# The matmuls of two dense layers as pairs on 64-column tiles of the array, side by side in one bank

## The chip, the cores and the metric

The kernel runs on one core of one Trainium2 chip. The metric is the device time of that core in microseconds, taken over several executions; a profiled execution gives the trace. All runs told here are in the fast state, at a granted TensorE clock of 0.995 to 1.000. Ratios are the mean time of one kernel's fast runs over that of the other's of the same rounds, so not quite the ratio of the medians quoted beside them.

## The reference

A linear attention (keys and values projected from 1024 to 64 rows), then two dense layers with a hard-swish between them, over 8 x 1024 tokens:

```python
k_proj = np.einsum('ks,bhsd->bhkd', E, k)          # 8 batches, 8 heads, 1024 -> 64 rows, 64 wide
v_proj = np.einsum('ks,bhsd->bhkd', F, v)
attn = softmax(q @ k_proj.T / 8)
x = (attn @ v_proj)                                # as 8192 tokens x 512
h = x @ w_in                                       # 512 -> 2048
g = h * np.clip(h + 3.0, 0.0, 6.0) / 6.0
out = g @ w_out                                    # 2048 -> 512
```

## The kernel before

Each batch is two blocks of 512 tokens. For a block, the first layer makes 16 groups of 4 accumulating matmuls, the second layer 4 groups of 16. All take 128 rows, 128 columns and 512 moving columns; only the very last group is split into two of 256 moving columns. The attention of the next batch is put in between the groups, in small 64x64 matmuls.

```python
def h_part(h_ps, xT, t, fo, kos):                                     # first layer
    for ko in kos:
        nc.tensor.matmul(h_ps, w_in_sb[:, ko, fo * P:(fo + 1) * P], xT[:, ko, t, :],
                         start=(ko == 0), stop=(ko == KO - 1))
...
    o_ps = pmm()                                                      # second layer
    for fo in range(FO):
        nc.tensor.matmul(o_ps, g[:, fo, c * P:(c + 1) * P], w_out_sb[:, fo, :],
                         start=(fo == 0), stop=(fo == FO - 1))
        if fo % SB == SB - 1:
            yield                                                     # attention work may come here
```

The projection of keys and values already uses pairs of 64-column tiles, with two different moving operands:

```python
def project(self, alloc):
    ps = self.ps = alloc()
    for so in range(SO):
        for e in range(2):
            nc.tensor.matmul(ps[e * KP:(e + 1) * KP], ef_t[e][:, so, :],
                             kqv[self.b]["kv"[e]][:, :, so, :],
                             start=(so == 0), stop=(so == SO - 1))
```

The softmax here doesn't subtract the row's maximum and nothing guards it: scores larger than these inputs give would overflow.

Of the kernel before, what the change touches and what calls it, by code (L numbers as in the profile page):

```python
# [15 lines left out]
def kernel(  # L16
# [11 lines left out]
    nc = tc.nc  # L28
# [5 lines left out]
    P = 128  # L34
    SO = S // P
    KO = d_model // P
    FO = d_ff // P
# [28 lines left out]
    def pmm():  # L66
        return ps_mm.tile([P, TOK], f32, tag="mm", name="mm")
# [5 lines left out]
    def g_tile():  # L73
        return gpool.tile([P, FO, TOK], bf16, tag="g", name="g")
# [51 lines left out]
    w_in_sb = consts.tile([P, KO, d_ff], bf16, name="w_in_sb")  # L126
    w_out_sb = consts.tile([P, FO, d_model], bf16, name="w_out_sb")
# [7 lines left out]
    for i in range(SB):  # L135
        c = slice(i * FO // SB, (i + 1) * FO // SB)
# [355 lines left out]
                nc.vector.tensor_mul(self.xT[:, j, 1, :], av[j], self.recs[j // 2][:, j % 2])  # L492


    def h_part(h_ps, xT, t, fo, kos):
        for ko in kos:
            nc.tensor.matmul(h_ps, w_in_sb[:, ko, fo * P:(fo + 1) * P], xT[:, ko, t, :],  # L497
                             start=(ko == 0), stop=(ko == KO - 1))

    def h_out(h_ps, g, fo):  # L500
        r = rpool.tile([P, TOK], f32, tag="r", name="r")
# [3 lines left out]
    def first_group(xT, t, g, fo):  # L505
        h_ps = pmm()
        h_part(h_ps, xT, t, fo, range(KO))
        h_out(h_ps, g, fo)

    def out_rows(b, t, c):  # L510
        return out_v[b, :, SB * t + 2 * (c % 2) + c // 2, :]


    def second_group(b, t, g, c, copy=None):
        o_dst = out_rows(b, t, c)
        if (b, t, c) == (B - 1, NB - 1, SB - 1):

            for e, copy, dma in ((0, nc.vector.tensor_copy, nc.sync), (1, nc.scalar.copy, nc.scalar)):
                half = slice(e * d_model // 2, (e + 1) * d_model // 2)
                o_ps = pmm()[:, :d_model // 2]  # L520
                for fo in range(FO):
                    nc.tensor.matmul(o_ps, g[:, fo, c * P:(c + 1) * P], w_out_sb[:, fo, half],  # L522
                                     start=(fo == 0), stop=(fo == FO - 1))
                o_sb = opool.tile([P, d_model], f32, tag="o_sb", name="o_sb")[:, :d_model // 2]
                copy(o_sb, o_ps)
                dma.dma_start(out=o_dst[:, half], in_=o_sb)
            return
        o_ps = pmm()
        for fo in range(FO):
            nc.tensor.matmul(o_ps, g[:, fo, c * P:(c + 1) * P], w_out_sb[:, fo, :],  # L530
                             start=(fo == 0), stop=(fo == FO - 1))
            if fo % SB == SB - 1:
                yield
        o_sb = opool.tile([P, d_model], f32, tag="o_sb", name="o_sb")
        (copy or nc.scalar.copy)(o_sb, o_ps)  # L535
        nc.sync.dma_start(out=o_dst, in_=o_sb)
# [5 lines left out]
    def x_tile():  # L542
        return xpool.tile([P, KO, NB, TOK], bf16, tag="xT", name="xT")


    xT = x_tile()
# [3 lines left out]
    g = [g_tile(), g_tile()]  # L550


    def two_groups(xT, t, g, kos):
        tiles = [pmm(), pmm()]
        for part in kos:
            for fo in range(2):
                h_part(tiles[fo], xT, t, fo, part)
        for fo in range(2):
            h_out(tiles[fo], g, fo)
# [10 lines left out]
    def pop():  # L570
        if later:
            later.pop(0)()

    rows = [second_group(0, 0, g[0], c) for c in range(SB)]
    for i in range(SB + 1):
        for c in range(SB - 1):
# [12 lines left out]
    for c in range(SB):  # L589
        for i, _ in enumerate(second_group(0, 1, g[1], c, nc.vector.tensor_copy)):  # L590
            pop()
            if i == 0:
                rest.append(second.visit(c, None))
            elif i == 2 or c == SB - 1:
                while rest:
                    rest.pop()()
    qT_dma[2] = q_transposed(2)
    xT = x_next
# [4 lines left out]
    for b in range(1, B):  # L603
# [33 lines left out]
        for t in range(NB):  # L637
            if b == 1 and t == 1:
                qT_dma[3] = q_transposed(3)
            g = g_tile()  # L640
            for fo in range(FO):
                if b < 3 and t == 0 and fo < 2:

                    if fo == 0:
                        two_groups(xT, t, g, ((0, 1, 2), (3,)))
                else:
                    first_group(xT, t, g, fo)
                pop()
                if b == 1 and t == 0 and fo == 10:
                    second.projected()  # L650
                if not behind or fo % SB < SB - 1:
                    continue
                inside, after = visits(b, t * SB + fo // SB)
                rows = second_group(*behind[0], fo // SB, nc.vector.tensor_copy if b == 1 else None)
                next(rows)
                next(rows)
                rest = inside()
                whole(rows)
                after()
                if rest:  # L660
                    rest()
            behind = [(b, t, g)]
        second, xT = third, x_next
# [32 lines left out]
```

## Time and profile before

| | before |
|---|---|
| time, median of the first 3 runs | 507.6 us (507.38 to 507.77) |
| span of the profile | 506.0 us |
| TensorE busy, granted clock | 98%, 0.999 |
| matmuls of the two layers (by the loops) | 1024 + 1008 + 32 short ones |
| start to start in a run of them | 0.216 us (0.110 us for the short ones) |
| share of the chain that ended last | 43% + 43% + 1% |

The distance from one start to the next is called the pitch here; it is shorter than the 379 ns that one matmul is recorded with, because neighbours overlap in the records. One more number of the kernel before is needed later, the stretch in the chain where nothing but the layers is left: it began at 424.83 us and the last matmul ended at 502.69, 77.86 us later. In the page, these lines are the matmuls of the two layers and the weight loads of the first: line, engine and operation, the tile of the array, the shapes and the count, then busy us and mean ns of one, then idle time before them.

```profile
L497 PE MATMUL mm<-xT,w_in_sb 128*128 128x512 bf16 x998 | 229.2, 379 | 1.5
L530 PE MATMUL mm<-w_out_sb,g 128*128 128x512 bf16 x985 | 227.8, 379 | 1.9 <-issue 1.0
...
L497 PEld LDWEIGHTS <-w_in_sb 128*128 128x128 bf16 x1024 | 99.6, 98 | 121.8 <-issue 3.3
```

The counts of matmuls are a few short of 1024 and 1008: some matmul records are missing in this trace.

### The profile page before, as it was taken

How to read it: one execution, taken by the hardware profiler on the slowest of the kernel's cores; microseconds unless marked ns; L12 is line 12 of the kernel's file. 1: busy time of each engine (PE TensorE's matmuls, PEld its weight loads, DVE VectorE, ACT ScalarE, POOL GpSimd, SP SyncE). 2: the span in 40 equal slices, each digit the busy share in tenths (PEclk: the TensorE clock that was granted, in tenths of full speed). 3: DMA queues.
4: the chain of work that ended last, by engine and by line, in shares of the span. 5: the costliest groups of instructions: out<-in, count | busy, mean ns of one | idle time of the engine just before them, and what ended most of it. 6: DMA issues, size and time to landing. Idle time of an engine off the chain costs nothing.

```text
span 506.0 us, 7034 instructions
## 1 busy us (share of the span) xinstructions
PE 495.5 (98%) x2729; PEld 225.1 (44%) x2779; DVE 245.1 (48%) x384; ACT 256.3 (51%) x438; POOL 37.9 (8%) x57
## 2 busy tenths in 40 slices
PE   8899999999999999999999999999999999999997
PEld 4444444444444444444444444444444444444444
DVE  3582736865733564536635455533752446334420
ACT  3656466567564444654555544654455544434431
POOL 8610020020020020010002000000000000000000
PEclk9999999999999999999999999999999999999999
DMA  9999999599299988699317990248110361101112
GB/s 166 199 205 207 202 157 234 109 149 199 79 152 193 264 149 172 137 159 251 113 43 134 216 263 26 63 97 209 41 43 32 79 162 43 41 22 42 43 42 84
DMA packets 77530, 66.04 MB, mean 131 GB/s; under 512 B 36200, under 2 KB 66664, under 8 KB 77496
## 3 DMA queue, kind: packets, MB, share of 16 engines
q0 software_dynamic: 31952, 29.36, 37.1%
q1 hardware_dynamic: 45320, 35.82, 27.0%
q10 hardware_dynamic: 224, 0.39, 0.3%
q8 instruction: 22, 0.36, 0.3%
q14 instruction: 12, 0.10, 0.1%
HBM read 69.73 MB, written 16.94 MB: 171 GB/s over the span
## 4 chain that ended last, share of the span: by engine, by line
PE 94%; DMA 2%; POOL 2%; issue 1%; ACT 1%; DVE 0%; ACTq 0%; POOLq 0%
PE mm L530 43%; PE mm L497 43%; PE at L195 2%; DMA v<-in_v_dram 2%; PE at L244 1%; PE at L226 1%; PE mm L244 1%; PE mm L522 1%; POOL q L106 1%; PE mm L264 1%; POOL k L110 1%; ACT aT L235 0%; PE mm L226 0%; POOL v L110 0%; PE mm L195 0%
## 5 line engine op out<-in xcount | busy, mean ns | idle before, releaser
L503 DVE SCALAR_TENSOR_TENSOR g<-r,mm 128x512 bf16<-128x512 f32 x256 | 173.6, 687 | 179.1 <-ACT r L502 178.3
L497 PE MATMUL mm<-xT,w_in_sb 128*128 128x512 bf16 x998 | 229.2, 379 | 1.5
L530 PE MATMUL mm<-w_out_sb,g 128*128 128x512 bf16 x985 | 227.8, 379 | 1.9 <-issue 1.0
L502 ACT ACTIVATE r<-mm 128x512 f32<-128x512 f32 x256 | 152.3, 599 | 74.5 <-PE mm L497 73.2
L497 PEld LDWEIGHTS <-w_in_sb 128*128 128x128 bf16 x1024 | 99.6, 98 | 121.8 <-issue 3.3
L530 PEld LDWEIGHTS <-g 128*128 128x128 bf16 x1008 | 96.7, 98 | 120.5 <-issue 7.4
L535 ACT COPY o_sb<-mm 128x512 f32<-128x512 f32 x55 | 32.3, 587 | 126.6 <-PE mm L530 126.6
L257 DVE TENSOR_TENSOR xT<-at,rec 128x512 bf16<-128x512 f32 x42 | 26.5, 682 | 6.5 <-ACT rec L176 6.5
L235 ACT ACTIVATE aT<-at 128x512 bf16<-128x512 f32 x38 | 20.2, 615 | 9.1 <-PE at L226 9.1
L201 DVE CAST kp<-at 64x512 bf16<-64x512 f32 x12 | 7.7, 677 | 15.5 <-PE at L195 15.5
L216 POOL COPY mark<-qT 1x1 bf16<-1x1 bf16 x4 | 0.7, 176 | 161.2 <-DMA qT<-q 161.2
L235 ACT ACTIVATE aT<-mm 128x512 bf16<-128x512 f32 x18 | 10.3, 613 | 3.6 <-PE mm L226 3.6
L535 DVE COPY o_sb<-mm 128x512 f32<-128x512 f32 x8 | 5.5, 688 | 13.4 <-PE mm L530 13.4
L195 PE MATMUL at<-k,e_t 128*64 128x512 bf16 x48 | 11.5, 382 | 0.0
L195 PE MATMUL at<-v,f_t 128*64 128x512 bf16 x48 | 11.5, 382 | 0.0
L257 DVE TENSOR_TENSOR xT<-mm,rec 128x512 bf16<-128x512 f32 x14 | 9.0, 685 | 4.3 <-PE mm L244 4.3
L176 ACT ACTIVATE rec<-rec 128x1024 f32<-128x1024 f32 x10 | 10.6, 1060 | 0.3
L170 ACT ACTIVATE rec<-mm 128x512 f32<-128x512 f32 x10 | 5.5, 595 | 7.9 <-PE mm L244 5.4
L170 ACT ACTIVATE few<-mm 128x512 f32<-128x512 f32 x10 | 5.4, 595 | 7.4 <-PE mm L264 7.4
L93 PE MATMUL mm<-ones 128*128 128x512 bf16 x18 | 7.4, 546 | 1.5 <-DVE halves L84 1.5
L204 DVE CAST vp<-at 64x512 bf16<-64x512 f32 x12 | 8.3, 694 | 0.4
L195 PEld LDWEIGHTS <-e_t 128*64 128x64 bf16 x56 | 5.6, 109 | 6.6 <-issue 1.9
(75 smaller groups left out, 160.5 us busy)
## 6 DMA issues: line engine op xcount, KB each, us to landing
out_dram<-o_sb SPq DMA_DIRECT2D x63, 256.0 KB, 2.5
rec<-rows SPq DMA_DIRECT2D x40, 256.0 KB, 6.3
k<-in_k_dram POOLq DMA_DIRECT2D x7, 1024.0 KB, 14.9
v<-in_v_dram POOLq DMA_DIRECT2D x7, 1024.0 KB, 20.7
q<-in_q_dram POOLq DMA_DIRECT2D x7, 1024.0 KB, 10.6
w_out_sb<-in_moe_w_out_dram POOLq DMA_DIRECT2D x4, 512.0 KB, 16.9
k<-in_k_dram POOLq DMA_DIRECT2D x4, 256.0 KB, 5.5
v<-in_v_dram POOLq DMA_DIRECT2D x4, 256.0 KB, 7.8
```

What stands on the lines that cost most here:

```text
L170: nc.scalar.activation(rec[:, i], den, AF.Ln)
L176: nc.scalar.activation(flat, flat, AF.Exp, scale=-1.0)
L195: nc.tensor.matmul(ps[e * KP:(e + 1) * KP], ef_t[e][:, so, :], kqv[self.b]["kv"[e]][:, :, so, :], start=(so == 0), stop=(so == SO - 1))
L204: nc.vector.tensor_copy(self.vp[a * KP:(a + 1) * KP], self.ps[KP:].rearrange("p (h d) -> p h d", d=D))
L235: nc.scalar.activation(self.aT[j][:, r].rearrange("p a n -> p (a n)"), tiles[r], AF.Exp, scale=scale)
L244: nc.tensor.matmul(tiles[t][c:c + D].rearrange("p (r n) -> p r n", r=2), stationary(r, 2 * j + a), self.aT[j][r:r + KP, :, a, :], start=Tr ...
L257: nc.vector.tensor_mul(self.xT[:, j, t, :], av[t], rec[:, t])
L497: nc.tensor.matmul(h_ps, w_in_sb[:, ko, fo * P:(fo + 1) * P], xT[:, ko, t, :], start=(ko == 0), stop=(ko == KO - 1))
L502: nc.scalar.activation(r, h_ps, AF.Relu, bias=0.5, scale=1.0 / 6.0)
L503: nc.vector.scalar_tensor_tensor(g[:, fo, :], r, 1.0, h_ps, op0=ALU.min, op1=ALU.mult)
L530: nc.tensor.matmul(o_ps, g[:, fo, c * P:(c + 1) * P], w_out_sb[:, fo, :], start=(fo == 0), stop=(fo == FO - 1))
L535: (copy or nc.scalar.copy)(o_sb, o_ps)
```

## The change

The intent is to have the two halves of a stationary operand as separate 64-column tiles, each with its own weights, so that the array can work on both at once, as it does in the projection, where the two of a pair start within 0.01 us of each other and pairs follow at 0.215 us (trace of the kernel before). Only the way in which a matmul is written changes; banks, order and evictions stay.

```diff
+    def halved(ps, stationary, moving, **flags):
+        for e in range(2):
+            nc.tensor.matmul(ps[e * P // 2:(e + 1) * P // 2], stationary[:, e * P // 2:(e + 1) * P // 2], moving,
+                             **flags)
+
     def h_part(h_ps, xT, t, fo, kos):
         for ko in kos:
-            nc.tensor.matmul(h_ps, w_in_sb[:, ko, fo * P:(fo + 1) * P], xT[:, ko, t, :],
-                             start=(ko == 0), stop=(ko == KO - 1))
+            halved(h_ps, w_in_sb[:, ko, fo * P:(fo + 1) * P], xT[:, ko, t, :],
+                   start=(ko == 0), stop=(ko == KO - 1))
...
-            nc.tensor.matmul(o_ps, g[:, fo, c * P:(c + 1) * P], w_out_sb[:, fo, :],
-                             start=(fo == 0), stop=(fo == FO - 1))
+            halved(o_ps, g[:, fo, c * P:(c + 1) * P], w_out_sb[:, fo, :],
+                   start=(fo == 0), stop=(fo == FO - 1))
```

(The same edit in the last, split group.)

More of the change, by code (lines that the diff above doesn't have):

```diff
@@ L521, in second_group @@
                 for fo in range(FO):
-                    nc.tensor.matmul(o_ps, g[:, fo, c * P:(c + 1) * P], w_out_sb[:, fo, half],
-                                     start=(fo == 0), stop=(fo == FO - 1))
+                    halved(o_ps, g[:, fo, c * P:(c + 1) * P], w_out_sb[:, fo, half],
+                           start=(fo == 0), stop=(fo == FO - 1))
                 o_sb = opool.tile([P, d_model], f32, tag="o_sb", name="o_sb")[:, :d_model // 2]
@@ L529, in second_group @@
         for fo in range(FO):
-            nc.tensor.matmul(o_ps, g[:, fo, c * P:(c + 1) * P], w_out_sb[:, fo, :],
-                             start=(fo == 0), stop=(fo == FO - 1))
+            halved(o_ps, g[:, fo, c * P:(c + 1) * P], w_out_sb[:, fo, :],
+                   start=(fo == 0), stop=(fo == FO - 1))
             if fo % SB == SB - 1:
```

## The prediction

The forecast's sum came to 507.6 - 0.25 = 507.35 us. That the instructions of L149 were not prepared ahead was not shown; the 31 ns stand as measured.

> **What bounds the kernel now.** I read the page's busy shares and the clock row first, then the chain that ended last, then the groups by line, and then the timeline around the few places where the kernel already does what the change wants to do everywhere.
>
> ```profile
> span 506.0 us, 7034 instructions
> PE 495.5 (98%) x2729; PEld 225.1 (44%) x2779; DVE 245.1 (48%) x384; ACT 256.3 (51%) x438; POOL 37.9 (8%) x57
> ...
> PEclk9999999999999999999999999999999999999999
> ...
> PE 94%; DMA 2%; POOL 2%; issue 1%; ACT 1%; DVE 0%; ACTq 0%; POOLq 0%
> ```
>
> TensorE is busy from end to end at full granted clock, and it is 94% of the chain; no other engine is over 51%. By line, the chain is 43% second-layer matmuls (L530), 43% first-layer ones (L497) and 0.7% the last group (L522). So the time is the number of matmuls of the two layers times the pitch at which they start. The pitch cannot be read from the mean of one instruction (379 ns), since neighbours overlap; it is read from a run of them in the chain in order of time:
>
> ```profile
> 60.75 3.45 PE mm L530 x16
> ...
> 489.96 9.23 PE mm L530 x42
> 499.19 3.51 PE mm L522 x32
> ```
>
> 3.45/16 = 0.216 us for a 512-column matmul, 3.51/32 = 0.110 us for a 256-column one. By the loops of the kernel there are 16 token blocks x 16 x 4 = 1024 first-layer matmuls, 63 x 16 = 1008 second-layer ones, and 32 short ones. 2032 x 0.216 + 32 x 0.110 = 442 us, 87% of the span, as the chain says. The change is worth what it does to 0.216 and 0.110.
>
> The place to learn that from is the projection (L195): it already runs pairs of 128-row, 64-column matmuls, one into partitions 0 to 63 and one into 64 to 127 of one bank.
>
> ```profile
> 262.38 0.40 PE L195 MATMUL at<-k,e_t 128*64 128x512 bf16 x1
> 262.38 0.40 PE L195 MATMUL at<-v,f_t 128*64 128x512 bf16 x1
> 262.62 0.38 PE L195 MATMUL at<-k,e_t 128*64 128x512 bf16 x1
> 262.62 0.38 PE L195 MATMUL at<-v,f_t 128*64 128x512 bf16 x1
> 262.83 0.38 PE L195 MATMUL at<-k,e_t 128*64 128x512 bf16 x1
> 262.84 0.38 PE L195 MATMUL at<-v,f_t 128*64 128x512 bf16 x1
> ...
> 263.91 0.38 PE L195 MATMUL at<-k,e_t 128*64 128x512 bf16 x1
> 263.92 0.38 PE L195 MATMUL at<-v,f_t 128*64 128x512 bf16 x1
> 264.23 1.04 PE L497 MATMUL mm<-xT,w_in_sb 128*128 128x512 bf16 x3
> ```
>
> The two of a pair start within 0.01 us of each other, and pairs follow at (263.91 - 262.62)/6 = 0.215 us. A pair costs what one full-width matmul costs. The last line shows the price of changing shape: 264.23 - 263.91 = 0.32 us to the next start, about 0.10 over the usual pitch.
>
> [...] a load of 128 columns is recorded with 98 ns, one of 64 columns with 109 ns, so halving the columns shortens nothing. [...]
>
> **The change part by part.**
> 1. Removed: 2064 matmuls and 2064 weight loads of 128 columns. Added: 4128 matmuls and 4128 loads of 64 columns, on the same moving data, bank and order. By the L195 pitch, a pair is 0.216 us where the single one was 0.216: 2032 x 0 = 0. The short ones have 256 columns; 64-wide tiles with 256 columns exist in the scores (L226), in waves about 0.10 us apart, so 32 x 0 = 0.
> 2. Weight loads: in L195 the loads of the next pair stand beside the running pair, and the two of a pair start together, 0.11 us each. They fit into 0.216 us even one after the other (0.218, just), and in the last group two at once fit into 0.110. Cost 0.
> 3. Evictions, PSUM buffers, transfers: the same banks, released by the second half, which ends about 4 ns after the first. 0.004 us where an eviction is waited for, which TensorE does hardly at all (its idle time over L497 and L530 is 3.4 us in all). Under 0.1 us.
> 4. Changes of shape. The seven projections no longer change shape when the layers follow: 7 x 0.10 = -0.7 us; three of them also enter from a layer matmul: 3 x 0.10 = -0.3. The PE-side query transposes inside the first block's layers (L394, two groups, 128 columns wide) now change shape going in and out: 4 x 0.10 = +0.4. Changes between the layers and the 64x64 attention tiles stay as they are in number (about 30 each way). The first pair after a change takes 262.62 - 262.38 = 0.24 us where a full-width matmul takes about 0.23: 35 x 0.01 = +0.35. Sum: -0.25 us.
> 5. Issue. Four instructions per 0.216 us, one each 54 ns, where it was one each 108. [...] the 32 instructions of an L195 run don't prove a rate for 442 us. Two places do better. Line L149 comes after a wait that the sequencer itself handles (the event at about 6.5 us in that line's list)[...]:
>
> ```profile
> 6.59 0.58 PEld L149 LDWEIGHTS <-g 128*128 128x128 bf16 x8 [0.74 <-ACT g L145]
> 6.60 0.71 PE L149 MATMUL at<-ident,g 128*128 128x128 bf16 x8
> ...
> 7.09 0.16 PEld L93 LDWEIGHTS <-ones 128*128 128x128 bf16 x2
> ```
>
> Eight loads and eight matmuls start between 6.59 and 7.09: 0.50/16 = 31 ns each. That is a rate of at least one per 31 ns where 54 is needed[...]. And the last group issues 64 instructions in 3.51 us, 55 ns each, with no gap. Cost 0.
> 6. Instruction fetch: queue q8 moves 22 packets, 0.36 MB, 0.3% of the transfer engines; some 4100 more instructions on 7034 make that perhaps 0.6%. Cost 0.
>
> Sum: 507.6 - 0.25 = 507.35, say 507.4 us.
>
> **The rivals.**
> - The tiles don't overlap, because here both halves read the very same moving columns, which no pair in the trace does (L195 reads k and v; L226 and L244 read neighbouring columns of one tile, or other partitions). If the second read waits for the first, each pair takes 0.43 us: + 442 us, about 950. If it only loses some cycles, anything between. For it: no direct evidence either way. Against: streams from two tensors and from near columns of one tensor all run at full pitch, so neither the same partitions nor the same tile collide. I give 3%.
> - Issue becomes the bound in a long run. [...] For it: the four-instruction stream has never had to last longer than 32 instructions. Against: the 31 ns of L149. [...] I give 5%.
> - Weight loads [...] no longer hide in a long stream: 2 x 0.109 = 0.218 against 0.216, plus 2032 x 0.002 = 4 us, and in the last group 32 x 0.108 = 3.5 us: about 515, still within 2%. Against: L195 shows the two loads starting together. I give 5%.
> - It gets faster[...]. Against: full-width matmuls already stand at the pitch of their columns, and PE idles 3.4 us over both lines; even all of that is 0.7%. A gain over 2% would need 10 us, which no row holds. I give 1%.
>
> **Range and chances.** The three runs before lie within 0.4 us. With the sum at -0.25 and errors of a few tenths in it, the main case is 506.5 to 508.5; the weight-load rival stretches the upper end. Point 507.4, eight in ten from 506.2 to 510. Faster by over 2% 0.01, within 2% 0.90, slower 0.09 (issue 5, same data 3, unknown 1).
>
> **What would show it right or wrong.** In the changed profile the two layers' groups should show about twice as many matmuls of 128*64, mean still near 379 ns; in the timeline the two of a pair a few ns apart, pairs 0.215 us apart; loads of 64 columns near 109 ns; TensorE still 98% busy at clock 9, 94% of the chain. VectorE and ScalarE rows should not move. Runs of the layers into L195 should lose their 0.10 us. If pairs stand 0.43 us apart, the shared moving data was it[...]; if the last group alone stretches past 3.5 us, the weight loads. [...]

## The result, and the profile after

| | before | after |
|---|---|---|
| time, median of 4 runs | 507.49 us (507.23 to 507.77) | 507.26 us (507.16 to 507.36) |
| ratio of fast runs | | 0.9993 (95%: 0.9978 to 1.0008) |
| span of the profile | 506.0 us | 505.6 us |
| instructions in the profile | 7034 | 11210 |

4,100 more instructions and no change of the time that is clear of the noise. The changed kernel was run once more in a later round, with 507.59 us (5 runs) against 507.79 us (8 runs) and a ratio of 1.0000 (0.9986 to 1.0014).

The page of the changed kernel, the lines that answer to those of before: busy shares, clock, the instruction queue, chain, and the groups of the two layers. All matmuls of the layers now have line L498, the helper's.

```profile
span 505.6 us, 11210 instructions
PE 498.4 (99%) x4842; PEld 258.5 (51%) x4843; DVE 245.2 (48%) x384; ACT 256.4 (51%) x438; POOL 37.9 (7%) x57
...
PEclk9999999999999999999999999999999999999999
...
q8 instruction: 38, 0.62, 0.5%
...
PE 94%; DMA 2%; POOL 2%; ACT 1%; issue 0%; DVE 0%; ACTq 0%; POOLq 0%
...
L498 PE MATMUL mm<-w_out_sb,g 128*64 128x512 bf16 (+1 forms) x2080 | 234.7, 376 | 0.2 <-DVE g L509 0.2
L498 PE MATMUL mm<-xT,w_in_sb 128*64 128x512 bf16 x2048 | 231.0, 379 | 0.1
L498 PEld LDWEIGHTS <-g 128*64 128x64 bf16 x2080 | 116.4, 110 | 105.2 <-issue 7.0
```

Twice as many matmuls, each recorded as long as before (379 ns), and yet nearly the same busy time (231 us against 229): busy time is the time covered, and the two of a pair lie on top of each other. A load of 64 columns is recorded with 110 ns, one of 128 columns before with 98; the row of loads rises only from 44% to 51%, for the same reason.

The chain in order of time (start, us, what, how many) shows the pitch over a long stretch. This is the end of the changed kernel:

```profile
424.43 77.88 PE mm L498 x752
```

752 matmuls are 376 pairs, 32 of them short: 344 x 0.216 + 32 x 0.110 = 77.8 us. The same stretch of the kernel before took 77.86 us. So a pair costs what one matmul cost, to 0.1%, also over 752 matmuls, and although both halves now read the same moving columns.

What remains is in the changes of tile shape. In the timeline (start, us, engine and line, tiles, shapes, count) the projection now stands among layer matmuls of its own shape:

```profile
163.83 0.38 PE L195 MATMUL mm<-v,f_t 128*64 128x512 bf16 x1
164.04 1.25 PE L498 MATMUL mm<-w_out_sb,g 128*64 128x512 bf16 x10
```

The layer follows after 164.04 - 163.83 = 0.21 us, where it was 0.32 (264.23 - 263.91 in the prediction's lines). The two executions did not reach their first layer matmul at the same time, though nothing before it was changed (first the kernel before, then the changed one):

```profile
21.04 1.25 PE L497 MATMUL mm<-xT,w_in_sb 128*128 128x512 bf16 x5
```

```profile
20.84 3.43 PE L498 MATMUL mm<-xT,w_in_sb 128*64 128x512 bf16 x30
```

So the effect of the change is counted from there (last column, from unrounded starts):

| start of | before | after | difference | from the first layer matmul on |
|---|---|---|---|---|
| first layer matmul | 21.04 | 20.84 | -0.20 | |
| first projection | 55.27 | 55.48 | +0.21 | +0.40 |
| first scores of the second batch | 68.45 | 68.53 | +0.08 | +0.27 |
| scores near 201 us | 201.53 | 201.29 | -0.24 | -0.03 |
| scores near 322 us | 321.67 | 321.29 | -0.38 | -0.19 |
| last products near 424 us | 424.21 | 423.80 | -0.41 | -0.21 |

The trace of the later round of the changed kernel has its first layer matmul at 21.02 us, and from there on +0.40, +0.27, -0.03, -0.19 and -0.22: the same within 0.01 us. The loss comes from the transposes in the first 36 us, the gain in steps at the projections.

### The profile page after: what moved, and what is told of

Same layout as the page of the kernel before. It is cut to its first block, busy times and chain, and to the rows that moved or that the text cites. A ratio compares the mean times of both kernels' runs of the same rounds, so it can differ in the third digit from the quotient of the medians.

```text
span 505.6 us, 11210 instructions
## 1 busy us (share of the span) xinstructions
PE 498.4 (99%) x4842; PEld 258.5 (51%) x4843; DVE 245.2 (48%) x384; ACT 256.4 (51%) x438; POOL 37.9 (7%) x57
## 4 chain that ended last, share of the span: by engine, by line
PE 94%; DMA 2%; POOL 2%; ACT 1%; issue 0%; DVE 0%; ACTq 0%; POOLq 0%
PE mm L498 87%; PE at L195 2%; DMA v<-in_v_dram 2%; PE at L244 1%; PE at L226 1%; PE mm L244 1%; POOL q L106 1%; PE mm L264 1%; POOL k L110 1%; ACT aT L235 0%; PE mm L226 0%; POOL v L110 0%; PE mm L195 0%; PE at L414 0%; PE at L394 0%
## 5 line engine op out<-in xcount | busy, mean ns | idle before, releaser
L498 PE MATMUL mm<-w_out_sb,g 128*64 128x512 bf16 (+1 forms) x2080 | 234.7, 376 | 0.2 <-DVE g L509 0.2
L498 PE MATMUL mm<-xT,w_in_sb 128*64 128x512 bf16 x2048 | 231.0, 379 | 0.1
L498 PEld LDWEIGHTS <-g 128*64 128x64 bf16 x2080 | 116.4, 110 | 105.2 <-issue 7.0
L498 PEld LDWEIGHTS <-w_in_sb 128*64 128x64 bf16 x2048 | 116.3, 110 | 104.7 <-issue 0.8
```

The lines of the kernel that those rows point to most:

```text
L498: nc.tensor.matmul(ps[e * P // 2:(e + 1) * P // 2], stationary[:, e * P // 2:(e + 1) * P // 2], moving, **flags)
```

## The experiments

A time that stays the same has more than one explanation: each cost is nil, or a gain and a loss cancel. And "a pair costs what one did" has to be explained, too: by what do the two overlap, and how far does that carry? My theory was that the tiles run as two independent lanes, each at its own pitch, that loads and issue hide, and that only changes of shape cost. The rivals: sharing the moving columns or standing next to each other in program order makes the pair free; the sequencer is near its limit; the loads are near theirs.

### One layer alone: what a change of shape costs

```diff
-            halved(o_ps, g[:, fo, c * P:(c + 1) * P], w_out_sb[:, fo, :],
-                   start=(fo == 0), stop=(fo == FO - 1))
+            nc.tensor.matmul(o_ps, g[:, fo, c * P:(c + 1) * P], w_out_sb[:, fo, :],
+                             start=(fo == 0), stop=(fo == FO - 1))
```

(and the same in the last group)

> Only the first layer's matmuls as pairs on 64-column tiles; the second layer full width again. My theory (pairs are free, a change of tile shape costs about 0.10 us plus 0.01 to 0.02 us in the first matmul after it): the two layers alternate, and the trace of the kernel before records 103 direct changes between them; 103 x 0.11 us = +11.5 us, so about 518.7 us, and gaps of 0.31 us at each change in place of 0.216. Rival [...]: 507.3 us, same as both kernels.

Measured: 519.56 us (4 runs) against 507.66 us, ratio 1.0241 (1.0219 to 1.0264), correct. The timeline of this run, where a first-layer run (64 columns) is followed by a second-layer run (128) and again by a first-layer run:

```profile
58.83 2.11 PE L498 MATMUL mm<-xT,w_in_sb 128*64 128x512 bf16 x18
60.87 3.63 PE L536 MATMUL mm<-w_out_sb,g 128*128 128x512 bf16 x16
64.43 1.92 PE L498 MATMUL mm<-xT,w_in_sb 128*64 128x512 bf16 x16
```

A piece ends when its last matmul does, 0.38 us after that one's start. So the last start of the first piece is 58.83 + 2.11 - 0.38 = 60.56, and the next shape starts 0.31 us later; the same for 64.12 to 64.43. The rival was that the lost time hides where two long matmuls meet and only the short attention tiles pay it. It falls: here two long matmuls meet, and the start comes after 0.31 us where 0.216 is usual. Halving one layer alone costs 2.4%; halving both costs nothing that these runs resolve. The expected 518.7 us was 0.9 us short.

### Four tiles of 32 columns: the issue

```diff
-        for e in range(2):
-            nc.tensor.matmul(ps[e * P // 2:(e + 1) * P // 2], stationary[:, e * P // 2:(e + 1) * P // 2], moving,
+        for e in range(4):
+            nc.tensor.matmul(ps[e * P // 4:(e + 1) * P // 4], stationary[:, e * P // 4:(e + 1) * P // 4], moving,
                              **flags)
```

> Every matmul of the two layers as four matmuls on 32-column tiles: eight instructions per 512 columns, one each 27 ns. Theory A (the sequencer delivers one instruction each 31 ns [...] as after the stall at 385.7 us of the changed kernel, where the second of a pair starts 31 ns after the first): 8 x 31 = 0.248 us per four where 0.216 was, 2032 x 0.032 + 32 x (0.248 - 0.110) = +69 us, about 577 us, pitch 0.248 us in the timeline. Theory B (the sequencer is not limited at 31 ns over long runs, the array's columns stay the bound): 507 us, same. Theory C (weight loads of 32 columns, at about 94 ns each, cannot overlap four at a time): 4 x 0.094 = 0.376 us per four, about +325 us.

Measured: 508.81 us against 507.66, ratio 1.0024 (1.0000 to 1.0049), correct. A and C fall, B stands. The end of the chain, the same stretch as above:

```profile
425.26 77.88 PE mm L498 x1504
```

Twice the matmuls again, in the same 77.88 us. In its last 3.5 us stand 128 matmuls of 256 moving columns and 128 loads, 14 ns for one instruction. At 31 ns they would need 7.9 us, and the 3008 instructions of the whole stretch 93 us. So the 31 ns that I had read as the sequencer's rate was only an upper limit, and the change, with one instruction each 54 ns, has at least a factor of two in hand: the quarters kept one each 27 ns through the whole run. Whether the 14 ns could last as long is not shown. The profiled span is 0.8 us longer than the changed kernel's. That fits the projections, which are 64 columns wide and again change shape on both sides; I did not test that by itself.

### The order within the pair: runs of two and of four

The same matmuls, in runs on one tile: lower, lower, upper, upper (AABB), and AAAABBBB.

```diff
-        for ko in kos:
-            halved(h_ps, ...)
+        for i in range(0, len(ks), RUN):                 # RUN = 2 or 4
+            for e in range(2):
+                cols = slice(e * P // 2, (e + 1) * P // 2)
+                for k in ks[i:i + RUN]:
+                    stationary, moving = operands(k)
+                    nc.tensor.matmul(ps[cols], stationary[:, cols], moving, start=(k == 0), stop=(k == last))
```

> The same in runs of two (AABB). My theory (tiles independent, started in program order): A1, then A2 with B1, then B2 with the next A1: two slots for two pairs, as many as side by side; 507.3 us, same, although the two that run together never share their moving columns. Rival (the pair is free only because its two halves share moving columns or are issued as neighbours of one position): between 728 us and 949 us.

> The same 64-column matmuls in another order: four on the lower tile, then four on the upper tile (AAAABBBB). My theory (each tile works through its own matmuls at 0.216 us, started in program order): only the fourth A with the first B and the fourth B with the next first A can overlap, six slots for four pairs: 1.5 x 442 us = +221 us, about 728 us. Rival 1 (the engine looks ahead and starts a B while As wait): 507 us. Rival 2 (no overlap unless the two share their moving columns): eight slots for four pairs, about 949 us.

Measured: runs of two 507.33 us, ratio 0.9993 (0.9976 to 1.0010); runs of four 507.67 us, ratio 0.9998 (0.9977 to 1.0020); both correct. Runs of four refute my theory, which expected 728 us: a matmul of the upper tile does start while earlier ones of the lower tile still wait. Runs of two came out at the time that I expected, but by luck, not by my theory. With starts in program order, the lower tile would run one matmul ahead of the upper, and where a first-layer group is followed by a second-layer one, a matmul of each layer would run together once. The trace of the runs of two shows the layers changing on both tiles at once:

```profile
57.13 3.62 PE L505 MATMUL mm<-xT,w_in_sb 128*64 128x512 bf16 x32
60.59 1.68 PE L505 MATMUL mm<-w_out_sb,g 128*64 128x512 bf16 x14
```

In neither trace, of runs of two or of four, do matmuls of different layers start within 0.15 us of each other. So A1 ran with B1 and A2 with B2, halves of one old matmul with the same moving columns, and these two runs do not test whether the pair must share them; the runs of eight below do. The question became how far ahead the engine can reach.

### Runs of eight and of sixteen: how far ahead

The second layer alone in runs of eight (the first stays at four), with the places for attention work after each run:

```diff
-        for first_fo in range(0, FO, SB):
-            in_runs(o_ps, range(first_fo, first_fo + SB), ...)
-            yield
+        for first_fo in range(0, FO, 8):
+            for e in range(2):
+                in_runs(o_ps, range(first_fo, first_fo + 8), ..., run=8, tiles=(e,))
+                yield
```

> The second layer in runs of eight on one tile (A x8, B x8), the first layer in runs of four as before. My strict order (one matmul after another, a later one may only start together with an earlier one) fell with the runs of four, which cost nothing. New theory, W2: instructions go in order into the tiles, and each tile holds one running matmul and one waiting; a B goes in as soon as the last A has become the waiting one. Then two slots overlap at each change of tile, a run of two or four loses nothing (4 - 2 = 2, 8 - 4 = 4 slots for four pairs), and a run of eight needs 16 - 4 = 12 slots for eight pairs: 1.5 times the second layer's 221 us, +110 us, about 617 us. W3 (two waiting): 10 slots, about 562 us. Rival, deep look-ahead [...]: 507 us, same. Strict order, for completeness: 14 slots, about 672 us.

Measured: 546.32 us, ratio 1.0759 (1.0736 to 1.0782), correct. None of the listed theories gives that. The timeline of this run shows why (the program has here four first-layer matmuls on the lower tile, four on the upper, and then eight second-layer ones on the lower and eight on the upper):

```profile
301.39 0.38 PE L503 MATMUL mm<-w_out_sb,g 128*64 128x512 bf16 x1
301.57 0.38 PE L503 MATMUL mm<-xT,w_in_sb 128*64 128x512 bf16 x1
301.60 0.38 PE L503 MATMUL mm<-w_out_sb,g 128*64 128x512 bf16 x1
301.79 0.38 PE L503 MATMUL mm<-xT,w_in_sb 128*64 128x512 bf16 x1
301.82 0.38 PE L503 MATMUL mm<-w_out_sb,g 128*64 128x512 bf16 x1
302.00 0.38 PE L503 MATMUL mm<-xT,w_in_sb 128*64 128x512 bf16 x1
302.03 2.14 PE L503 MATMUL mm<-w_out_sb,g 128*64 128x512 bf16 x13
```

At 301.39 a second-layer matmul starts, while three first-layer matmuls that come earlier in the program start only at 301.57, 301.79 and 302.00. They belong to the upper tile, which still works off its run; the lower one is free. So starts are out of program order between tiles, by up to three matmuls here. These lines also answer the rival about the moving columns: matmuls of two different layers, which share no operand, start 0.03 us apart and still follow each other at 0.216 us a pair. Four pairs ran at this change of tile (second-layer starts at 301.39, 301.60, 301.82 and 302.03); what sets the four was not tested. With as many at each change, a run of eight can just be covered in the steady part, but a stop for attention leaves four matmuls alone at the end of one run and four at the start of the next. In the trace, 289 matmuls of the layers have no other start within 0.15 us of theirs (in the changed kernel and in the runs of two and four there is none). Each takes a slot of 0.216 us where the share of one in a pair is 0.108: 289 x 0.108 = 31 us. The remaining 7 us are the steady part: there the distances of the starts repeat with 0.03 us more for every four pairs, 63 x 4 x 0.03 = 7.6 us.

That explanation was made from this run, so it needed one that could refute it:

```diff
-        for first_fo in range(0, FO, 8):
-            for e in range(2):
-                in_runs(o_ps, range(first_fo, first_fo + 8), ..., run=8, tiles=(e,))
-                yield
+        for e in range(2):
+            in_runs(o_ps, range(FO), ..., run=16, tiles=(e,))
+            yield
+        yield
+        yield
```

> The second layer in runs of sixteen on one tile, both runs ahead of the attention work that used to come in the middle of a group. W2, W3, strict order and deep look-ahead each missed the runs of eight (546 us). New theory from that trace, W4: a matmul of the other tile starts while up to three earlier ones of the first tile still wait, so four slots overlap at each change of tile; in the runs of eight the steady part then loses nothing but 0.03 us per four pairs (7.6 us), and each stop for attention leaves four matmuls alone on each side (0.86 us x some 36 = 31 us), together the 38.5 us measured. W4 for runs of sixteen: 16 of a group's 32 matmuls stand alone, each costs half a slot: 8 x 0.216 = 1.73 us for each of 63 groups = +109 us, +1.8 us for the last one, and some 35 stops at 0.43 us = +15 us: about 633 us. Rival, the look-ahead is deep and the 38 us of the runs of eight came from the stops alone: runs of sixteen ahead of the stops would then cost less than the runs of eight, under 546 us.

Measured: 660.12 us, ratio 1.3001 (1.2963 to 1.3038), correct. The rival falls, W4 stands in kind: in the steady part of the trace four pairs, then eight single starts 0.216 us apart, then four pairs, and so on. Six of the single starts, in a view that ends at 613 us: (1.46 - 0.38)/5 = 0.216 us.

```profile
611.79 1.46 PE L503 MATMUL mm<-w_out_sb,g 128*64 128x512 bf16 x6
```

My sum was short by 27 us. The trace has 1263 matmuls alone, not the 16 x 63 + 35 x 4 = 1148 that I had worked with: after a stop the first run of the next group has no partner for 12 matmuls in place of 8. 1263 x 0.108 = 136 us, with 63 x 2 x 0.03 = 4 us in the overlaps. Of the other 12 us, 10 are 26 longer gaps between starts of layer matmuls, counted beyond 0.216 us, the largest of 1.2 to 1.9 us before 43 us, where TensorE waited among other things for the weights of the second layer (3.8 us in its list of waits). So a single 64-column matmul takes the full 0.216 us; only the second lane makes a pair free.

### Half the moving columns: the loads

```diff
-        for e in range(2):
-            nc.tensor.matmul(ps[e * P // 2:(e + 1) * P // 2], stationary[...], moving, **flags)
+        n = moving.shape[-1] // 2
+        for m in range(2):
+            for e in range(2):
+                nc.tensor.matmul(ps[e * P // 2:(e + 1) * P // 2, m * n:(m + 1) * n], stationary[...],
+                                 moving[:, m * n:(m + 1) * n], start=start and m == 0, stop=stop and m == 1)
```

> Each pair split again along the moving columns: four matmuls of 64 columns by 256 moving columns, so eight instructions for what was two, and two weight loads of 64 columns in each 0.110 us. If loads of 64 columns (recorded 0.110 us) on the two tiles really run together, and the sequencer keeps up with 27 ns per instruction as it did with quarters: 4 x 0.110 / 2 = 0.220 us per old matmul against 0.216: 1008+1024 times 0.003 = +6 us at most, 507 to 514 us. If the two loads take turns: 2 x 0.110 = 0.220 per 256 columns, 0.44 per old matmul: +450 us. If the pitch has a fixed part per matmul of 2 to 3 ns, 0.2185 per old matmul: +5 us, 512 us.

Measured: 513.51 us, ratio 1.0115 (1.0093 to 1.0136), correct. The last stretch of the chain:

```profile
430.70 78.82 PE mm L500 x1504
```

0.94 us more than with 512 columns, spread over 344 old matmuls: 2.7 ns each, with the short ones, split as well, in it. That is near what the fixed part per matmul gives: in the last 40 us of this trace pairs start 0.1092 us apart on average, and twice that is 0.2183, less 0.2158 in the changed kernel: 2.5 ns, or 5.1 us over 2032 old matmuls. The loads of 64 columns, two in every 0.11 us, run together on the two tiles; in turns they would have doubled the time. The 5.7 us in all need not be this alone. In the profiled execution, the slowest of the four, a projection that began at 203.84 us stood still until its values had landed:

```profile
206.04 0.38 PE L195 MATMUL at<-v,f_t 128*64 128x512 bf16 x1 [1.79 <-DMA v<-in_v_dram]
```

### The transposes halved too

The one loss that the prediction charged to the change was at the transposes within the first block's layers. They can be halved as well:

```diff
-                        nc.tensor.transpose(ps[:, o:o + P],
-                                            q0[:, t, 2 * j + a, 2 * m:2 * m + 2, :].rearrange("p s d -> p (s d)"),
-                                            ident)
+                        for e in range(2):
+                            nc.tensor.transpose(ps[e * D:(e + 1) * D, o:o + P], q0[:, t, 2 * j + a, 2 * m + e, :], ident)
```

> The changed kernel once more, as it is, as the yardstick for the run with halved transposes on the same chip: 507.3 us, ratio to before 0.9990 to 1.0000, span 505.5 us.

> The changed kernel with the query transposes of the first block also as two on 64-column tiles, so that the layers around them no longer change tile shape. Prediction's step 4: four changes of 0.10 us go, -0.4 us, and the pairs of transposes cost what one did: span about 505.1 us against 505.5 of the changed kernel, time 506.9 us. In the timeline the first transposes after a layer matmul follow at 0.216 us in place of 0.31, and the layer matmul after them at 0.06 in place of 0.15. Rival: a transpose on 64-column tiles does not run two at a time; then 16 transposes at 0.056 us more, +0.9 us, about 508 us, less the 0.4.

Measured in the same rounds: the change again 507.59 us, ratio to before 1.0000 (0.9986 to 1.0014); with halved transposes 507.30 us (6 runs), ratio 0.9989 (0.9976 to 1.0003); both correct. The spans are 505.7 and 505.6 us. The two intervals overlap: no gain is shown. The local part came as expected. The timeline around the transposes, first of the changed kernel, then with halved ones:

```profile
33.91 0.62 PE L394 MATMUL at<-ident,q 128*128 128x128 bf16 x8
34.46 1.05 PE L498 MATMUL mm<-xT,w_in_sb 128*64 128x512 bf16 x8
```

```profile
33.65 0.61 PE L395 MATMUL at<-ident,q 128*64 128x128 bf16 x16
34.10 1.03 PE L497 MATMUL mm<-xT,w_in_sb 128*64 128x512 bf16 x8
```

From the first transpose to the next layer matmul it is 0.55 us with one shape change, 0.45 us without. Sixteen transposes on half the columns take no longer than eight (0.61 against 0.62 us). But the chain of this run says where the gain went:

```profile
27.16 28.17 DMA v<-in_v_dram
...
55.37 1.89 PE at L195 x15
```

The values of the second batch landed at 27.16 + 28.17 = 55.33 us. The first projection, now ready at 54.86 us, waited for them in its second matmul until 55.37. In the changed kernel the same transfer was not waited for; its chain has no transfer at this place:

```profile
49.82 5.83 PE mm L498 x54
55.65 1.73 PE at L195 x16
```

Its values had landed at 54.67 us, by the semaphore that the projection waits for (54.53 in the later round, 54.45 in the kernel before), before the first projection started at 55.48. So the landing was late in this one execution; that the start is bound by a transfer in general is not shown. Some 13 us later one more transfer was late. The first scores read `qT`, and their semaphore came at 68.46 us, just before they started at 68.59, where it came at 67.02 in the changed kernel. A marker that waits for the same transfer shows it in the profile (68.51, where it is 67.07 in the changed kernel):

```profile
68.51 0.18 POOL L216 COPY mark<-qT 1x1 bf16<-1x1 bf16 x1 [37.97 <-DMA qT<-q]
```

Counted from the first layer matmul as in the table above, the halved transposes did bring the expected gain: -0.05 us against the kernel before at the first projection, where the changed kernel has +0.40. The two waits, 0.50 us and 0.18 us (a gap of 0.49 us where a change of shape takes 0.31), then took it away: +0.50 at the first scores, where the changed kernel has +0.27. One trace does not say how often they come.

## Why the prediction was right, by its own steps

- **Step 1, a pair costs what one matmul cost:** shown, 77.88 us against 77.86 us for the same stretch. The risk named among the rivals, that both halves read the same moving columns, did not come true in the change itself. Sharing them is not needed either: in the runs of eight, matmuls of different layers run together, 0.03 us apart, at the same 0.216 us a pair.
- **Step 2, weight loads:** shown. 110 ns each, hidden at 0.216 us a pair; and with two in every 0.11 us (half the moving columns) still hidden, at 0.1092 us a pair. They do overlap between the tiles, as the projection had suggested. The fallback in that step, that they fit even one after the other, was a slip: 0.218 us does not fit into 0.216, as the rival says itself.
- **Step 3, evictions and buffers:** VectorE and ScalarE rows moved by 0.1 us each.
- **Step 4, changes of shape:** the sum of -0.25 us agrees with the measured -0.23 and -0.20 us of the two sets of runs, but both are inside the noise of the times. The traces say more. Counted from the first layer matmul, both traces of the changed kernel stand at -0.21 and -0.22 us at 424 us, and their parts come near the prediction's: the transposes cost 0.45 us (+0.40 in the changed kernel against -0.05 with halved ones, at the first projection), where the prediction has 0.4; from the first projection to 424 us the traces give -0.61 and -0.62 us, where its other terms, without the entry into that first projection, have about -0.7 - 0.2 + 0.35 = -0.55. The unit cost is shown by the run with one layer halved (+12 us for 103 recorded changes, 0.12 us each, of which 0.095 us in the gap itself).
- **Step 5, issue:** right in its conclusion, loose in its number. I read 31 ns per instruction from the transposes after a wait; the quarters keep 27 ns through the run, and 14 ns over the last 3.5 us. Issue was not the bound: in the quarters one matmul started each 54 ns through the run, and 128 in the last 3.5 us, 27 ns each, while four of 512 columns still took 0.216 us.
- **Step 6, instruction fetch:** 0.3% of the transfer engines before, 0.5% after; no wait on it.

What the prediction did not know is why the pair is free. It only had the projection's pattern, and my theory for the experiments added to it that matmuls start in program order. The runs of four (ratio 0.9998, no matmul alone) show a wider freedom, and those of eight (289 alone) and sixteen (1263 alone) its limit: in these runs the two tiles worked as two lanes, each at 0.216 us per matmul of 512 columns, with four pairs at a change of tile and no more. Why it was four stays open.

## What to carry to other kernels

In this kernel the full-width matmuls already stood at 0.216 us each, and cutting them into column tiles neither gained nor lost: a pair took the same 0.216 us. What counted was to keep one tile shape, since each change cost 0.10 us or a little more, and to keep the tiles' turns close in program order: up to four matmuls in a row on one tile were free within the noise, while runs of eight in one layer cost 7.6% and runs of sixteen 30%. Before two traces are compared by their times, look for a place that nothing changed and count from there: two executions of these kernels differed by 0.2 us before their first layer matmul. Look for the cheapest place in the kernel that already does what a change wants to do everywhere; eight pairs in a projection gave this answer before anything was built.
